# Expansion tiles of one or two PSUM banks out of one four-bank ring, in the first phase of a ConvNeXt-V2 block

## Chip, cores, metric

One core of one Trainium2 chip. The metric is the device time of one execution in microseconds (us), median of several runs. Each experiment is compared with runs of the kernel before that were taken beside it, so the median of before differs a little from place to place (1559.86 to 1561.48 us). "TensorE", "ScalarE", "VectorE" and "POOL" are the engines that the profile calls PE, ACT, DVE and POOL; SP issues transfers.

## The reference

```python
# x: [1, 512, 512, 96], dw: [3, 3, 96], w1: [96, 384], w2: [384, 96], all bf16
out = depthwise_3x3(x, dw)
h = layernorm(out, axis=-1)
h = gelu(einsum('bhwc,ce->bhwe', h, w1))
gx = sqrt((h * h).sum(axis=(1, 2)) + 1e-6)          # over the whole image
nx = gx / (gx.mean(axis=-1) + 1e-6)
h = grn_gamma * (h * nx) + grn_beta + h
return x + einsum('bhwe,ec->bhwc', h, w2)
```

The sum of squares over the whole image cuts the kernel in two. Phase 1 makes the convolution, the layer norm, the expansion to 384 channels and the gelu, and gathers the sums. Phase 2 makes the second product and the output. The change touches phase 1 only.

## The kernel before

The image is worked through in 128 blocks of four rows. One slot of the phase-1 loop does the convolution of one block and the expansion of an earlier one. A helper records every instruction in program order on its engine, so nearly every profile line names line 32 of the kernel; the tile names tell the lines apart.

The kernel's matmuls put their results into tiles in PSUM. The kernel lays it out as eight banks of 512 f32 per partition (in the trace, `Y` is 128x1536 f32 and a `U` 128x1024 f32): one for the statistics (`SG`, with the layer norm sums `S` and the Gram sums), three for the convolution (`Y`, a single buffer), four for the expansions (`U`, two buffers of two banks).

```python
psS = tile_pool(name="psS", bufs=1, space=PSUM)      # SG
psU = tile_pool(name="psU", bufs=2, space=PSUM)      # U: two tiles of two banks
psY = tile_pool(name="psY", bufs=1, space=PSUM)      # Y: three banks
# ... cut
def burst(n, fence=True):                            # a third of the convolution: 24 matmuls of 64 rows x 32 columns
    # ... cut: matmuls into Y
    if n < 2 and fence:
        pe.drain()

def evac():                                          # frees Y
    act.activation(out=y[:], in_=Y3[:], func=Identity)
# ... cut
def pair(j):                                         # two banks of the expansion, one gelu
    U = psU.tile([128, 2, QW], f32, name="U")
    for t in range(2):
        cm_mm(U[:, t, :], j, t)                      # 128x128 weights, 512 columns
    act.activation(out=gsh[:, :, j, :], in_=U[:], func=Gelu_apprx_tanh)
# rest(n): two banks as well, into gm; squares(j): bn_stats of a gelu's output on VectorE

conv(0); pair(0); conv(1); spread_out(); turn_x(s + 2)
pair(1); squares(0); gram_of_last(0)
pair(2); squares(1); gram_of_last(1)
rest(0); squares(2); conv(2); evac()
rest(1); stage_stats(b2)
rest(2); squares_rest()
```

So a slot has three conv bursts, six gelus over two banks each and one evacuation over three banks. A framework turns uses of tiles into semaphore waits; nothing in the kernel writes a wait by hand.

Of the kernel before, what the change touches and what calls it, by code (L numbers as in the profile page):

```python
# [53 lines left out]
def kernel(  # L54
# [20 lines left out]
    NI = C // 32  # L75
# [12 lines left out]
    def is_res(q):  # L88
        return q >= NBLK - RES
# [70 lines left out]
    with ExitStack() as p1:  # L160
# [2 lines left out]
        gmpool = p1.enter_context(tc.tile_pool(name="gm", bufs=3))  # L163
        bstpool = p1.enter_context(tc.tile_pool(name="bst", bufs=2))
        psS = p1.enter_context(tc.tile_pool(name="psS", bufs=1, space=bass.MemoryType.PSUM))
        psU = p1.enter_context(tc.tile_pool(name="psU", bufs=2, space=bass.MemoryType.PSUM))
        pc = p1.enter_context(ExitStack())
        psY = pc.enter_context(tc.tile_pool(name="psY", side="right", bufs=1, space=bass.MemoryType.PSUM))
        xinpool = pc.enter_context(tc.tile_pool(name="xin", side="right", bufs=4))
# [84 lines left out]
        def recompute_units(q):  # L254
            nk = kept_quads(q)
            ynt = grp[q]["ynt"]

            def fresh(j):
                if j == 0:
                    grp[q]["made"] = late.gr.tile([128, NCH, (NQ - 1) * QW], bf16, name="gr")  # L260
                if is_res(q):
                    U = psU.tile([128, 2, QW], f32, name="U")
                else:
                    U = late.psU2.tile([128, NQ - 1, QW], f32, name="U2")
                for t in range(nk, NQ):
                    pe.matmul(quad_out(U[:, t - nk, :]), lhsT=w1p[:, j * 128:(j + 1) * 128],
                               rhs=quad(ynt[:], t), start=True, stop=True)
                n = (NQ - nk) * QW
                act.activation(out=grp[q]["made"][:, j, :n], in_=U[:].rearrange("p k w -> p (k w)")[:, :n],
                                func=ACTF.Gelu_apprx_tanh)  # L270

            return [lambda j=j: fresh(j) for j in range(NCH)]
# [69 lines left out]
                pe.matmul(J[:, k % NI, :], lhsT=zrow[:, :128], rhs=zrow[:], start=True, stop=True)  # L342

        busy(FILL[0])
        Ud = psU.tile([128, 2, W], f32, name="U")[:, 0, :NI * 9].rearrange("p (i k) -> p i k", i=NI)
        for i in range(NI):
            dve.tensor_copy(out=dwx[:, i], in_=dw9[:, None, chans(i)].to_broadcast([9, GR, 32]))
            pe.matmul(Ud[:, i, :], lhsT=dwx[:, i].rearrange("p q c -> p (q c)"), rhs=ident_b[:9, :9],
# [38 lines left out]
        def turn_x(b):  # L387
            xin = xins.pop(b)
            t = xt_ring[b % NXT]
            pairs = t[:, 0:2, :].rearrange("p i s -> p (i s)").bitcast(f32)  # L390
            dve.transpose(out=pairs.rearrange("p (g m) -> p g m", m=MB),
                          in_=xin[:, :, 0:64].bitcast(f32))
            dve.transpose(out=t[:, 2, :].rearrange("p (g m) -> p g m", m=MB), in_=xin[:, :, 64:96])
# [13 lines left out]

        def conv_taps(b, spare):
            if spare:
                Ua = psU.tile([128, 2, W], f32, name="U")  # L410
                Ub = psU.tile([128, 2, W], f32, name="U")
                Y = [Ua[:, 0, :], Ua[:, 1, :], Ub[:, 0, :]]
            else:
                Y3 = psY.tile([128, NI, W], f32, name="Y")
                Y = [Y3[:, i, :] for i in range(NI)]
            mms = []
            for n in range(3):
                mms.append([(h, j, (n + h) % NI, dx) for dx in (0, -1, 1) for j in range(GR) for h in range(2)])
            flat = [m for ms in mms for m in ms]
            first = {}  # L420
            last = {}
            for n, (h, j, i, dx) in enumerate(flat):
                first.setdefault((i, j), n)
                last[i, j] = n

            def burst(n, fence=True):
                k = sum(len(ms) for ms in mms[:n])
                for h, j, i, dx in mms[n]:
                    src = b + shift(h, j)
                    o0, o1 = max(0, -dx), W - max(0, dx)  # L430
                    pe.matmul(
                        Y[i][32 * j:32 * j + 32, o0:o1],
                        lhsT=Wq[64 * h:64 * h + 64, i, dx + 1, j, :],
                        rhs=x_rows(src, 64 * h, 64 * h + 64, i, MB * (1 + dx) + o0, o1 - o0)
                        if 0 <= src < NBLK else zrow[64 * h:64 * h + 64, o0:o1],
                        start=first[i, j] == k,
                        stop=last[i, j] == k,
                    )
                    k += 1
                if n < 2 and fence:  # L440
                    pe.drain()

            def evac():
                y = ypool.tile([128, NI, W], bf16, name="y_bf")
                if spare:
                    act.activation(out=y[:, 0:2, :], in_=Ua[:], func=ACTF.Identity)
                    act.activation(out=y[:, 2, :], in_=Ub[:, 0, :], func=ACTF.Identity)
                else:
                    act.activation(out=y[:], in_=Y3[:], func=ACTF.Identity)
                ybf[b] = y  # L450

            return [lambda fence=True, n=n: burst(n, fence) for n in range(3)], evac
# [83 lines left out]
        def stage_spread(k):  # L536
            n = BATCHES[k][1]
            wide = rns.pop(k)
            U = psU.tile([128, 2, W], f32, name="U")
            for bb in range(n):  # L540
                for g in range(NG):
                    pe.matmul(U[:, bb, g * 128:(g + 1) * 128],
                              lhsT=wide[:, bb, g].rearrange("p j c -> p (j c)"), rhs=ident_b[:],
                              start=True, stop=True)
            rbc = rbcpool.tile([128, BATCH, W], bf16, name="rbc")
            act.activation(out=rbc[:, :n, :], in_=U[:, :n, :], func=ACTF.Identity)
            rbcs[k] = rbc
# [63 lines left out]
        def mlp_units(b):  # L611
# [4 lines left out]
            def cm_mm(dst, j, t):  # L616
                pe.matmul(quad_out(dst), lhsT=w1p[:, j * 128:(j + 1) * 128], rhs=quad(yt[:], t), start=True, stop=True)

            def pair(j):
                U = psU.tile([128, 2, QW], f32, name="U")  # L620
                for t in range(2):
                    cm_mm(U[:, t, :], j, t)
                act.activation(out=gsh[:, :, j, :], in_=U[:], func=ACTF.Gelu_apprx_tanh)

            def rest(n):
                U = psU.tile([128, 2, QW], f32, name="U")
                Uf = U[:].rearrange("p k w -> p (k w)")
                c0 = 2 * QW * n
                c, end = c0, c0 + 2 * QW
                while c < end:  # L630
                    if c < px0(b):
                        j, sz = c // QW, QW
                        cm_mm(Uf[:, c - c0:c - c0 + sz], j, 2)
                    else:
                        k, e0 = divmod(c - px0(b), E)
                        sz = min(E - e0, 512 - c % 512, end - c)
                        t, r = divmod(k, GR)
                        col = (cm_quads(b) + t) * 128
                        pe.matmul(Uf[:, c - c0:c - c0 + sz], lhsT=yt[:, r, col:col + 128], rhs=w1p[:, e0:e0 + sz],
                                  start=True, stop=True)  # L640
                    c += sz
                act.activation(out=gms[b][:, c0:end], in_=Uf, func=ACTF.Gelu_apprx_tanh)
# [16 lines left out]
            def store():  # L659
                sp.dma_start(out=g_dram[b], in_=gsh[:, 0].rearrange("p j w -> p (j w)"))  # L660

            return pair, rest, squares, squares_rest, store

        def gram_mms(b, part=None):
            n = (TAIL - px0(b)) // E
# [56 lines left out]
        for s in range(last_slot + 1):  # L722
# [26 lines left out]
            def spread_out():  # L749
                for k in get("spread"):  # L750
                    stage_spread(k)
                for b in get("norma"):
                    stage_norm(b)
# [24 lines left out]
                    gram_mms(b)  # L778
            else:
                b = mlp[0]  # L780
                pair, rest, squares, squares_rest, put_out = mlp_units(b)
                conv = lambda n, fence=True: taps[n](fence) if taps else None

                def gram_of_last(part):
# [1 line left out]
                        if b2 != b:  # L786
                            gram_mms(b2, part)

                conv(0)
                pair(0)  # L790
                conv(1)
                spread_out()
                if s + 2 < NBLK:
                    turn_x(s + 2)
                pair(1)
                squares(0)
                if not taps:
                    gram_of_last(0)
                    gram_of_last(1)
                if taps:  # L800
                    gram_of_last(0)
                pair(2)
                squares(1)
                if taps:
                    gram_of_last(1)
                rest(0)
                squares(2)
                for k in get("turn"):
                    stage_turn(k)
                conv(2)  # L810
                if evac:
                    evac()
                rest(1)
                for b2 in get("stats"):
                    stage_stats(b2)
                rest(2)
                squares_rest()
                for b2 in get("gram"):
                    if b2 == b:
                        gram_mms(b2)  # L820
# [125 lines left out]
```

## Time and profile before

| | before |
|---|---|
| median (first 3 runs) | 1561.48 us |
| slots with convolution, evacuation to evacuation (median) | 7.40 us |
| last evacuation / first addition of phase 2 starts at | 934.9 us / 1027.3 us |
| granted TensorE clock, whole run | 0.991 |

The windows of 300 to 800 us, the kernel before: for each engine busy us and, in brackets, instructions; then the granted clock, the share of the DMA engines and GB/s.

```profile
300.00:800.00 500.00, 465.69 (x8223) 225.53 (x8216) 477.04 (x803) 465.38 (x469) 449.39 (x328) 1.00 0.77 236
```

The order is TensorE, weight loads, VectorE, ScalarE, POOL. TensorE and ScalarE are each idle for about 7%, VectorE for less than 5%. A kernel like this has no single bounding engine, so the waits come next. The waits of ScalarE and of TensorE in the same stretch (waiting engine and tile, what it waited for, us in total, times, longest):

```profile
ACT gsh L32 <- PE U L32: 34.5, 71, 1.5
```

```profile
PE Y L32 <- ACT y_bf L32: 13.4, 66, 0.4
PE SG L32 <- DVE SG L32: 5.0, 4, 1.6
```

ScalarE waits once a slot, in front of one gelu; TensorE waits once a slot, for the evacuation. One slot in the timeline (start, length, engine, instruction, count, and in brackets the idle time before and what ended it), ScalarE and then TensorE:

```profile
598.24 1.47 ACT L32 ACTIVATE y_bf<-Y 128x1536 bf16<-128x1536 f32 x1
599.57 1.97 ACT L32 ACTIVATE gm<-U 128x1024 bf16<-128x1024 f32 x2
601.45 1.02 ACT L32 ACTIVATE gsh<-U 128x1024 bf16<-128x1024 f32 x1
602.91 1.94 ACT L32 ACTIVATE gsh<-U 128x1024 bf16<-128x1024 f32 x2 [0.44 <-PE U L32]
604.74 1.03 ACT L32 ACTIVATE gm<-U 128x1024 bf16<-128x1024 f32 x1
605.64 1.47 ACT L32 ACTIVATE y_bf<-Y 128x1536 bf16<-128x1536 f32 x1
```

```profile
599.76 0.89 PE L32 MATMUL Y<-xT,Wq 64*32 64x512 bf16 x24 [0.20 <-ACT y_bf L32]
600.76 0.60 PE L32 MATMUL U<-ynT,w1p 128*128 128x512 bf16 x2
601.29 0.87 PE L32 MATMUL Y<-xT,Wq 64*32 64x512 bf16 x24
602.27 0.60 PE L32 MATMUL U<-ynT,w1p 128*128 128x512 bf16 x2
...
604.51 0.88 PE L32 MATMUL Y<-xT,Wq 64*32 64x512 bf16 x24
605.32 0.39 PE L32 MATMUL U<-ynT,w1p 128*128 128x512 bf16 x1
```

Read as a loop: the evacuation ends at 599.71, conv 0 starts at 599.76, the first pair at 600.76, conv 1 at 601.29, the second pair at 602.27. Its gelu starts at 602.91, and after two more gelus the next evacuation starts at 605.64 and ends at 607.11. That is 7.40 us. Conv 0 and conv 1, which end in a drain, take 1.00 and 0.98 us until the next instruction starts; conv 2, without one, takes 0.81.

### The profile page before, as it was taken

What the parts mean: (1) busy time and instruction counts of PE and PEld (TensorE: products, weight loads), DVE (VectorE), ACT (ScalarE), POOL (GpSimd) and SP (SyncE); (2) the same over time, 40 slices, a digit from 0 to 9 for tenths busy, and PEclk for the clock granted to TensorE, in tenths of its full rate; (3) what the DMA queues carried; (4) which work ended last, traced back from release to release, by engine and by line L of the source; (5) the groups of instructions that cost most, each with busy time, mean ns of one, the idle gap of its engine ahead of it and who ended that gap; (6) DMA issues with size and microseconds to landing.
All of it is one profiled execution on the core that took longest, in us unless ns stands there. A gap on an engine that the chain in (4) does not pass through costs nothing. (4 is left out here: it accounts for less than half of the span.)

```text
span 1559.3 us, 54608 instructions
## 1 busy us (share of the span) xinstructions
PE 1438.9 (92%) x23119; PEld 819.7 (53%) x23119; DVE 1211.7 (78%) x2157; ACT 1436.7 (92%) x1306; POOL 1318.4 (85%) x933
## 2 busy tenths in 40 slices
PE   7889989999999999999999997789999999999998
PEld 3334444444444444444444443357777766676666
DVE  6749989999999999999999999955555555455555
ACT  3779989999999999999999999999999999899997
POOL 3459889989998998898899897459999999899997
PEclk8899999999999999999999999999999999999999
DMA  5568787777778778778868767879999999999996
GB/s 152 162 174 256 241 251 249 223 225 246 228 245 250 231 226 258 237 221 250 244 207 252 221 198 222 275 249 395 380 385 384 381 377 378 341 389 379 376 379 236
DMA packets 235467, 427.86 MB, mean 274 GB/s; under 512 B 34103, under 2 KB 148375, under 8 KB 235223
## 3 DMA queue, kind: packets, MB, share of 16 engines
q1 hardware_dynamic: 219972, 356.59, 70.4%
q0 software_dynamic: 13888, 67.64, 11.5%
q8 instruction: 181, 2.97, 0.8%
q14 instruction: 64, 0.52, 0.1%
q10 hardware_dynamic: 1362, 0.15, 0.1%
HBM read 272.78 MB, written 150.72 MB: 272 GB/s over the span
## 5 line engine op out<-in xcount | busy, mean ns | idle before, releaser
L32 PE MATMUL U<-ynT,w1p 128*128 128x512 bf16 x2292 | 664.4, 381 | 48.5 <-ACT gm L32 10.0
L32 ACT ACTIVATE gr<-U 128x1536 bf16<-128x1536 f32 (+1 forms) x384 | 519.1, 1456 | 13.1 <-PE U L32 11.3
L32 DVE BATCH_NORM_STATS2 bst<-gsh 128x6 f32<-128x512 bf16 x756 | 463.0, 674 | 21.7 <-ACT gsh L32 15.7
L32 DVE TENSOR_TENSOR o_sb<-O,xb 128x384 bf16<-128x384 f32 x512 | 277.9, 556 | 250.7 <-PE O L32 153.0
L32 POOL TENSOR_TENSOR yn<-y_bf,rbc 128x1536 bf16<-128x1536 bf16 x128 | 397.4, 3107 | 87.3 <-ACT rbc L32 31.0
L32 ACT ACTIVATE gsh<-U 128x1024 bf16<-128x1024 f32 x378 | 374.5, 1025 | 61.5 <-PE U L32 61.4
L278 POOL TENSOR_TENSOR xb<-xr,B2c 128x1536 f32<-128x1536 bf16 x126 | 394.8, 3135 | 33.9 <-DVE B2c L32 30.9
L32 ACT ACTIVATE gm<-U 128x1024 bf16<-128x1024 f32 x384 | 381.8, 1047 | 0.2
L32 PE MATMUL Y<-xT,Wq 64*32 64x511 bf16 (+1 forms) x8694 | 324.6, 391 | 32.9 <-ACT y_bf L32 25.8
L32 POOL TENSOR_TENSOR ysq<-y_bf 128x1536 bf16<-128x1536 bf16 x114 | 313.2, 2748 | 32.9 <-ACT y_bf L32 32.4
L32 PEld LDWEIGHTS <-w1p 128*128 128x128 bf16 x2292 | 181.6, 97 | 289.5 <-issue 203.3
L32 PEld LDWEIGHTS <-gr 128*128 128x128 bf16 x4584 | 236.8, 98 | 107.5 <-issue 23.4
L32 PE MATMUL O<-W2s,gr 128*128 128x96 bf16 x4584 | 257.2, 206 | 12.4 <-DVE o_sb L32 11.9
L32 DVE BATCH_NORM_STATS2 bst<-gm 128x6 f32<-128x512 bf16 x378 | 242.3, 679 | 29.7 <-ACT gm L32 29.7
L32 PEld LDWEIGHTS <-Wq 64*32 64x32 bf16 x9216 | 114.0, 91 | 212.5 <-issue 174.1
L32 ACT ACTIVATE y_bf<-Y 128x1536 bf16<-128x1536 f32 x121 | 177.5, 1467 | 16.2 <-PE Y L32 16.1
L32 DVE STREAM_TRANSPOSE xT<-xin 128x576 f32<-128x576 f32 (+1 forms) x256 | 180.4, 745 | 2.1 <-DMA xin<-in_x_dram 2.0
L32 PEld LDWEIGHTS <-gm 128*128 128x128 bf16 x1560 | 106.8, 98 | 66.3 <-issue 11.7
L32 PE MATMUL SG<-gm 128*128 128x128 bf16 x1560 | 126.1, 219 | 8.9 <-DVE SG L32 8.2
L32 PE MATMUL U<-w1p,ynT 128*128 128x384 bf16 (+2 forms) x780 | 126.5, 272 | 5.0 <-ACT gm L32 3.8
L250 POOL DMA_DIRECT2D xr<-in_x_dram x123 | 68.4, 556 | 35.9 <-POOL xb L278 35.9
L32 PEld LDWEIGHTS <-ynT 128*128 128x128 bf16 x780 | 67.3, 97 | 35.3 <-issue 15.4
(103 smaller groups left out, 696.6 us busy)
## 6 DMA issues: line engine op xcount, KB each, us to landing
ynT<-yn_dram SPq DMA_DIRECT2D x254, 384.0 KB
xin<-in_x_dram SPq DMA_DIRECT2D x126, 432.0 KB
yn_dram<-yn SPq DMA_DIRECT2D x512, 96.0 KB
xr<-in_x_dram POOLq DMA_DIRECT2D x128, 384.0 KB, 6.5
out_dram<-o_sb SPq DMA_DIRECT2D x127, 384.0 KB
g_dram<-gsh SPq DMA_DIRECT2D x126, 384.0 KB
gl<-g_dram SPq DMA_DIRECT2D x84, 384.0 KB
gl<-g_dram POOLq DMA_DIRECT2D x42, 384.0 KB, 7.2
```

What stands on the lines that cost most here:

```text
L32: r = f(*a, **k)
L250: pq.dma_start(out=xr[:], in_=x[0, r0:r0 + GR].rearrange("r w c -> (r w) c").rearrange("(p g) c -> p g c", g=PXP))
L278: pq.tensor_tensor(out=xb[:], in0=grp[q]["xr"][:], in1=bias[:, None, :].to_broadcast([128, PXP, C]), op=ALU.add)
```

## The change

The intent is to keep the same four banks but hand them out singly. Three banks can then be expanded before conv 1, and ScalarE can start on one bank while TensorE fills the next. The slot becomes 2, 1, conv, 1, 2, 2, conv, evacuation, 2, 1, 1 (banks per gelu): eight gelus for six. The drain after conv 1 is dropped.

```diff
-        psU = p1.enter_context(tc.tile_pool(name="psU", bufs=2, space=bass.MemoryType.PSUM))
+        psU = p1.enter_context(tc.tile_pool(name="psU", bufs=1, space=bass.MemoryType.PSUM))
+        NB = 4
+        ring = psU.tile([128, NB, W], f32, name="U")
+        next_bank = [0]
+
+        def banks(n):
+            k = next_bank[0] % NB
+            if k + n > NB:
+                k = 0
+            next_bank[0] = k + n
+            return ring[:, k:k + n, :]
 ... every psU.tile([128, 2, ...]) becomes banks(2)
-            def pair(j):
-                U = psU.tile([128, 2, QW], f32, name="U")
-                for t in range(2):
-                    cm_mm(U[:, t, :], j, t)
-                act.activation(out=gsh[:, :, j, :], in_=U[:], func=ACTF.Gelu_apprx_tanh)
+            def unit(bank, n):
+                U = banks(n)
+                if bank < 2 * NCH:
+                    j, t0 = divmod(bank, 2)
+                    for t in range(t0, t0 + n):
+                        cm_mm(U[:, t - t0, :], j, t)
+                    act.activation(out=gsh[:, t0:t0 + n, j, :], in_=U, func=ACTF.Gelu_apprx_tanh)
+                    return
 ... (rest(n) becomes the other half of unit)
+                if taps:
+                    conv(0)
+                    unit(0, 2)
+                    unit(2, 1)
+                    squares(0)
+                    conv(1, False)
 ... spread_out, turn_x
+                    unit(3, 1)
+                    unit(4, 2)
+                    squares(1)
+                    gram_of_last(0)
+                    unit(6, 2)
+                    squares(2)
 ... turn
+                    conv(2)
+                    evac()
+                    gram_of_last(1)
+                    unit(8, 2)
+                    unit(10, 1)
+                    unit(11, 1)
+                    squares_rest()
 ... stage_stats; slots without convolution use six units of two banks
```

More of the change, by code (lines that the diff above doesn't have):

```diff
@@ L261, in fresh @@
                 if is_res(q):
-                    U = psU.tile([128, 2, QW], f32, name="U")
+                    U = banks(2)
                 else:
@@ L268, in fresh @@
                 n = (NQ - nk) * QW
-                act.activation(out=grp[q]["made"][:, j, :n], in_=U[:].rearrange("p k w -> p (k w)")[:, :n],
+                act.activation(out=grp[q]["made"][:, j, :n], in_=(U if is_res(q) else U[:]).rearrange("p k w -> p (k w)")[:, :n],
                                 func=ACTF.Gelu_apprx_tanh)
@@ L344 @@
         busy(FILL[0])
-        Ud = psU.tile([128, 2, W], f32, name="U")[:, 0, :NI * 9].rearrange("p (i k) -> p i k", i=NI)
+        Ud = banks(2)[:, 0, :NI * 9].rearrange("p (i k) -> p i k", i=NI)
         for i in range(NI):
@@ L409, in conv_taps @@
             if spare:
-                Ua = psU.tile([128, 2, W], f32, name="U")
-                Ub = psU.tile([128, 2, W], f32, name="U")
+                Ua, Ub = banks(2), banks(2)
                 Y = [Ua[:, 0, :], Ua[:, 1, :], Ub[:, 0, :]]
@@ L445, in evac @@
                 if spare:
-                    act.activation(out=y[:, 0:2, :], in_=Ua[:], func=ACTF.Identity)
+                    act.activation(out=y[:, 0:2, :], in_=Ua, func=ACTF.Identity)
                     act.activation(out=y[:, 2, :], in_=Ub[:, 0, :], func=ACTF.Identity)
@@ L538, in stage_spread @@
             wide = rns.pop(k)
-            U = psU.tile([128, 2, W], f32, name="U")
+            U = banks(2)
             for bb in range(n):
@@ L617, in cm_mm @@
                 pe.matmul(quad_out(dst), lhsT=w1p[:, j * 128:(j + 1) * 128], rhs=quad(yt[:], t), start=True, stop=True)
-            def pair(j):
-                U = psU.tile([128, 2, QW], f32, name="U")
-                for t in range(2):
-                    cm_mm(U[:, t, :], j, t)
-                act.activation(out=gsh[:, :, j, :], in_=U[:], func=ACTF.Gelu_apprx_tanh)
-            def rest(n):
-                U = psU.tile([128, 2, QW], f32, name="U")
-                Uf = U[:].rearrange("p k w -> p (k w)")
-                c0 = 2 * QW * n
-                c, end = c0, c0 + 2 * QW
+            def unit(bank, n):
[6 more added lines that the diff above has]
+                    return
+                Uf = U.rearrange("p k w -> p (k w)")
+                c = c0 = (bank - 2 * NCH) * QW
+                end = c0 + n * QW
                 while c < end:
@@ L660, in store @@
                 sp.dma_start(out=g_dram[b], in_=gsh[:, 0].rearrange("p j w -> p (j w)"))
-            return pair, rest, squares, squares_rest, store
+            return unit, squares, squares_rest, store
         def gram_mms(b, part=None):
@@ L780 @@
                 b = mlp[0]
-                pair, rest, squares, squares_rest, put_out = mlp_units(b)
+                unit, squares, squares_rest, put_out = mlp_units(b)
                 conv = lambda n, fence=True: taps[n](fence) if taps else None
@@ L787, in gram_of_last @@
                             gram_mms(b2, part)
-                conv(0)
-                pair(0)
-                conv(1)
-                spread_out()
-                if s + 2 < NBLK:
-                    turn_x(s + 2)
-                pair(1)
-                squares(0)
-                if not taps:
+                if taps:
[4 more added lines that the diff above has]
+                    conv(1, False)
+                    spread_out()
+                    if s + 2 < NBLK:
+                        turn_x(s + 2)
+                    unit(3, 1)
[4 more added lines that the diff above has]
+                    squares(2)
+                    for k in get("turn"):
+                        stage_turn(k)
+                    conv(2)
[5 more added lines that the diff above has]
+                    squares_rest()
+                    for b2 in get("stats"):
+                        stage_stats(b2)
+                else:
+                    unit(0, 2)
+                    unit(2, 2)
+                    spread_out()
@@ L798 @@
                     gram_of_last(0)
                     gram_of_last(1)
-                if taps:
-                    gram_of_last(0)
-                pair(2)
-                squares(1)
-                if taps:
-                    gram_of_last(1)
-                rest(0)
-                squares(2)
-                for k in get("turn"):
-                    stage_turn(k)
-                conv(2)
-                if evac:
-                    evac()
-                rest(1)
-                for b2 in get("stats"):
-                    stage_stats(b2)
@@ L816 @@
-                rest(2)
-                squares_rest()
+                    squares(0)
+                    unit(4, 2)
+                    squares(1)
+                    for k in get("turn"):
+                        stage_turn(k)
+                    unit(6, 2)
+                    squares(2)
+                    unit(8, 2)
+                    for b2 in get("stats"):
+                        stage_stats(b2)
+                    unit(10, 2)
+                    squares_rest()
                 for b2 in get("gram"):
```

## The prediction

> **What bounds the kernel now.** The activity table by slices shows two phases: blocks with a convolution until about 940 us, a tail of expansions without convolution until about 1010 us, then the output phase. The change touches the first two. In the timeline a steady block lasts 7.40 us (evacuation to evacuation; few differ by over 0.1 us). No engine is full: in the windows table from 140 to 940 us, VectorE is busy 94.7%, ScalarE 92.9%, POOL 89.8%, and the waits of ScalarE are nearly all one wait: 54.1 us in 113 waits, gelu of the second pair waiting for its matmuls, 0.44 us a block.
>
> That wait closes a loop which I can add up to the measured period: end of the evacuation of Y (one Y buffer) -> +0.05 conv 0 with its drain 1.00 -> first pair 0.53 -> conv 1 0.98 -> second pair 0.60 until its end -> +0.04 gelu 0.92, 0.91, 0.90 (starts to starts) -> evacuation 1.47 = 7.40 us. So a latency loop between TensorE and ScalarE is the limit.
>
> **What the change does.** It keeps four PSUM banks, but hands them out singly, so three banks (1.5 tiles) are expanded before conv 1, and the single banks let ScalarE start earlier. The loop becomes: 0.05 + conv 0 1.00 + three banks about 0.75 + conv 1 without its drain 0.81 (as conv 2 takes now) + one bank 0.39 + 0.04 + gelu 0.50 + 0.92 + 0.92 + evacuation 1.47 = 6.85 us, an estimate from the same rows. It adds two ACTIVATEs per block (8 for 6). [...]0.60 us for 512 elements, 1.02 for 1024, 0.92 from start to start. [...] The removed drain saves TensorE about 0.17 us (0.98 against 0.81); its floor is about 6.8. Matmuls, transfers, VectorE and POOL work stay; VectorE needs about 7.05 to 7.1 per block, POOL 6.8 with the gaps in its short chains.
>
> So the loop stops being the limit, and ScalarE, VectorE and nearly POOL come to theirs together. With bursts (aggregation 2.8 us per 11 blocks, moments once in 4) they do not all reach it: the wait of the Gram matmuls for VectorE's clearing of SG (7.5 us in all now) should grow. I expect 7.15 to 7.2 us, 0.25 us less, for about 113 blocks: 28 us. The tail without convolution (5.55 us a block) is already ScalarE-bound without gaps and keeps its tile sizes: no change.
>
> **Predicted: 1533 us**, 8 in 10 between 1516 and 1550. Chances: faster by over 2% 0.42, within 2% 0.55, slower by over 2% 0.03.
>
> **What would show it.** Steady block 7.1 to 7.2 us; the 0.44 us wait of ScalarE almost gone (under 15 us in all); ScalarE busy 97% or more in that stretch; single-bank gelus near 0.60 us; VectorE waits under 0.15 us a block. If the block stays at 7.3 or more and ScalarE waits moved to another gelu, bank waits or VectorE's backlog took the gain.
>
> **What would make it wrong.** The dependencies of the shared ring tile tracked coarser than by bank; a stall of TensorE once in four blocks that grows as VectorE lags[...].

The three durations are in the trace of before: 0.60 us for ACTIVATEs of 512 elements (`rbc<-U`, mean 598 ns), 1.02 for gelus of 1024 (`gsh<-U`, mean 1025 ns), 0.92 from start to start. The floors of TensorE, VectorE and POOL are estimates, close to their busy time of 742.14, 757.73 and 718.56 us in the 800 us from 140 to 940 us (6.86, 7.01 and 6.65 us in 7.40). The sum came to this: the loop falls to 6.85 us and no longer limits; by the floors, a slot takes 7.15 to 7.2 us; 0.25 us less in about 113 slots is 28 us, and 1561 less 28 is 1533 us.

## The result, and the profile after

Ratios are the mean time of one kernel's runs over the mean of the other's runs of the same rounds, so they are not quite the ratios of the medians that stand beside them. All outputs are right.

| | before | after |
|---|---|---|
| median | 1561.45 us (4 runs) | 2526.57 us (2513.58 to 2530.38, 4 runs) |
| ratio, 95% interval | | 1.617 (1.611 to 1.623) |
| evacuation to evacuation, median | 7.40 us | 15.7 us (quartiles 13.5 and 16.1) |
| last evacuation starts at | 934.9 us | 1796.9 us |
| first addition of phase 2 starts at | 1027.3 us | 1995.7 us |
| granted clock, whole run | 0.991 | 0.756 |

The change made the kernel 62% slower. Of the 968 us by which phase 2 starts later, 862 are lost up to the last evacuation and 106 in the slots without convolution that follow. Phase 2 itself takes as long as before.

The windows of 300 to 800 us, the changed kernel:

```profile
300.00:800.00 500.00, 345.89 (x4188) 136.45 (x4173) 250.38 (x401) 262.98 (x302) 223.41 (x163) 0.71 0.39 121
```

TensorE, VectorE and POOL ran about half as many instructions as before in the same 500 us (ScalarE, which has more and smaller gelus in a slot, 302 for 469), and ScalarE fell from 93% to 53% busy. The granted clock fell from 1.00 to 0.71. The waits of ScalarE and TensorE there:

```profile
ACT gsh L32 <- PE U L32: 156.3, 130, 3.2
ACT gm L32 <- PE U L32: 67.2, 100, 1.2
...
```

```profile
PE U L32 <- ACT gsh L32: 79.3, 99, 1.3
PE U L32 <- ACT gm L32: 70.8, 66, 1.7
```

The second fence points to the cause. Before, no expansion waited for a gelu in this stretch. Now TensorE waits 165 times for a gelu, in front of expansions (`PE U`), for 150 us. ScalarE waits for expansions 230 times, for 224 us. Two engines that each wait for the other's last instruction are taking turns. One slot shows it, ScalarE (the first three quarters of the slot) and then TensorE (the first half):

```profile
1004.26 1.02 ACT L32 ACTIVATE gsh<-U 128x1024 bf16<-128x1024 f32 x1 [2.62 <-PE U L32]
1005.96 0.60 ACT L32 ACTIVATE gsh<-U 128x512 bf16<-128x512 f32 x1 [0.68 <-PE U L32]
1007.91 0.60 ACT L32 ACTIVATE gsh<-U 128x512 bf16<-128x512 f32 x1 [1.35 <-PE U L32]
1009.61 1.02 ACT L32 ACTIVATE gsh<-U 128x1024 bf16<-128x1024 f32 x1 [1.10 <-PE U L32]
1011.78 1.02 ACT L32 ACTIVATE gm<-U 128x1024 bf16<-128x1024 f32 x1 [1.15 <-PE U L32]
```

```profile
1001.55 1.48 PE L32 MATMUL Y<-xT,Wq 64*32 64x512 bf16 x24
1003.15 1.03 PE L32 MATMUL U<-ynT,w1p 128*128 128x512 bf16 x2
1005.34 0.59 PE L32 MATMUL U<-ynT,w1p 128*128 128x512 bf16 x1 [1.16 <-ACT gsh L32]
1005.86 1.48 PE L32 MATMUL Y<-xT,Wq 64*32 64x512 bf16 x24
1007.27 0.61 PE L32 MATMUL U<-ynT,w1p 128*128 128x512 bf16 x1
1008.56 1.01 PE L32 MATMUL U<-ynT,w1p 128*128 128x512 bf16 x2 [0.69 <-ACT gsh L32]
```

The pair at 1003.15 fills banks 0 and 1. The single expansion at 1005.34 fills bank 2, which nothing holds. It nevertheless starts 0.06 us after the gelu of banks 0 and 1 ended (1004.26 + 1.02 = 1005.28). In the same way the pair at 1008.56 (banks 0 and 1) follows the end of the gelu of bank 3 at 1008.51.

The compiled program says the same. For each first matmul of an expansion, this is the bank it writes, and the gelu whose completion its semaphore wait names (one slot of the changed kernel, same order as in the code):

```
expansion writes bank   waits for the gelu that read bank
0, 1                    3        (needed: 0, 1, three gelus earlier)
2                       0, 1     (needed: 2)
3                       2        (needed: 3)
0, 1                    3
2, 3                    0, 1
0, 1                    2, 3
2                       0, 1
3                       2
```

Every expansion waits for the gelu just before it; in the trace of the slot, five of the eight waits can be seen, and the other three are hidden behind other matmuls (the gelus that they name end at 1001.64, 1006.56 and 1012.80 us, before TensorE comes to those expansions at 1003.15, 1007.27 and 1013.66). In the kernel before, every pair waits for the gelu two pairs back, the last reader of its own tile. So the framework seems to treat the ring as one object, which the experiments test: such a ring is a single buffer, however many banks it has. The waits guard the whole tile, not the bank in use.

There is a second difference between the two slots. The conv burst took 1.48 us for 0.89, and the pair 1.03 for 0.60. The windows of 2 us over this slot, the changed kernel, TensorE alone (length, busy and instructions, granted clock, DMA share, GB/s):

```profile
1002.00:1004.00 2.00, 1.88 (x26) 0.50 0.01 4
1006.00:1008.00 2.00, 1.88 (x25) 0.50 0.03 8
...
1016.00:1018.00 2.00, 1.31 (x36) 1.00 0.96 324
```

The clock is 0.50 or 1.00, and 0.50 for most of the slot (of the five windows left out, four have 0.50, and one that holds both has 0.84). This slot alone can't tell how much of the loss is the waiting and how much is the clock, nor which causes which.

### The profile page after: what moved, and what is told of

Read it like the earlier page. It is cut to its first block, busy times and chain, and to the rows that moved or that the text cites. A ratio compares the mean times of both kernels' runs of the same rounds, so it can differ in the third digit from the quotient of the medians.

```text
span 2527.2 us, 54724 instructions
## 1 busy us (share of the span) xinstructions
PE 1879.0 (74%) x23119; PEld 919.4 (36%) x23119; DVE 1259.5 (50%) x2157; ACT 1544.5 (61%) x1534; POOL 1318.0 (52%) x933
## 4 chain that ended last, share of the span: by engine, by line
PE 59%; ACT 26%; POOL 6%; issue 3%; DMA 3%; DVE 1%; SPq 1%; ACTq 0%; POOLq 0%
PE U L32 32%; PE Y L32 15%; ACT gsh L32 13%; ACT gm L32 9%; PE O L32 7%; POOL xb L289 5%; PE SG L32 5%; ACT y_bf L32 4%; DMA yn_dram<-yn 2%; SPq L32 1%; DVE o_sb L32 1%; POOL gl L256 1%; DMA ynT<-yn_dram 1%; DMA xin<-in_x_dram 0%; POOL xr L261 0%
## 5 line engine op out<-in xcount | busy, mean ns | idle before, releaser
L32 PE MATMUL U<-ynT,w1p 128*128 128x512 bf16 x2292 | 862.3, 465 | 351.6 <-ACT gsh L32 299.5
L32 DVE BATCH_NORM_STATS2 bst<-gsh 128x6 f32<-128x512 bf16 x756 | 489.4, 680 | 641.3 <-ACT gsh L32 637.4
L32 ACT ACTIVATE gsh<-U 128x1024 bf16<-128x1024 f32 x492 | 406.2, 826 | 593.9 <-PE U L32 586.2
L32 ACT ACTIVATE gm<-U 128x1024 bf16<-128x1024 f32 x498 | 412.3, 828 | 277.7 <-PE U L32 275.0
L32 PE MATMUL Y<-xT,Wq 64*32 64x511 bf16 (+1 forms) x8694 | 453.9, 530 | 9.6 <-DVE B2bc_f L32 3.7
L32 PEld LDWEIGHTS <-w1p 128*128 128x128 bf16 x2292 | 207.1, 107 | 545.8 <-issue 484.3
L32 PE MATMUL U<-w1p,ynT 128*128 128x384 bf16 (+2 forms) x780 | 167.7, 306 | 262.6 <-ACT gm L32 260.4
L32 PEld LDWEIGHTS <-ynT 128*128 128x128 bf16 x780 | 85.1, 109 | 361.9 <-issue 344.2
L32 PEld LDWEIGHTS <-gm 128*128 128x128 bf16 x1560 | 147.0, 130 | 135.0 <-issue 129.5
L32 PE MATMUL SG<-gm 128*128 128x128 bf16 x1560 | 185.2, 282 | 0.0
```

The costliest lines, as they stand in the source:

```text
L32: r = f(*a, **k)
```

## The experiments

Theory A: the ring tile is one object to the waits, so TensorE and ScalarE take turns, and the low clock follows from TensorE's idle time. Theory B: the new order, the smaller tiles or the missing drain cost the time; the ring is only storage. Theory C: the low clock is a cause of its own, or TensorE's load lowers it.

### ring_only: the ring without the new order

```diff
  # the kernel before, its order (2, conv, 2, 2, 2, conv, evacuation, 2, 2) and its drains kept
-        psU = tile_pool(name="psU", bufs=2, ...)
+        ring = psU.tile([128, 4, W], f32, name="U")      # banks(n) as in the change
-                U = psU.tile([128, 2, QW], f32, name="U")
+                U = banks(2)
```

> The kernel before with its own order and its pairs, only that the pairs are slices of one four-bank tile. Theory A (the ring tile is one object for the waits, so every expansion waits for the gelu just before it, whatever bank it uses): about as slow as the change, 2150 to 2450 us, the granted clock under 0.85, and TensorE waits of near 1 us for the gelu just before in front of most expansions. Theory B (the new order, the smaller tiles and the missing drain are what costs; the ring is only storage): within 2% of before, 1530 to 1590 us.

Measured: 2108.33 us (2 runs), ratio 1.350. The waits of TensorE from 300 to 800 us, this kernel:

```profile
PE U L32 <- ACT gsh L32: 78.7, 117, 0.8
PE U L32 <- ACT gm L32: 71.8, 117, 1.1
```

Order, tile sizes, number of gelus and drains are those of before; pairs go alternately to banks 0, 1 and 2, 3, as they did in the two tiles. Only the object is one. The same waits appear and a slot takes 10.9 us for 7.40. Theory B does not explain this run. The time fell just short of the range given, the waits are shorter than expected (0.6 to 0.7 us on the mean), and the clock is higher (0.911): the turn-taking is costly even with little loss of clock.

### split_tiles: the new order without the ring

```diff
+        def banks(n):
+            if n == 2: U = psU.tile([128, 2, W], f32, name="UA")
+            else:      U = psU.tile([128, 1, W], f32, name="UC" or "UD", in turn)
-                    unit(6, 2)
+                    unit(6, 1); unit(7, 1)                # a pair can't span two tiles
```

> The changed order and the dropped drain, but the four banks are three separate tiles: one of two banks, two of one bank; where the changed kernel put a pair on the two single banks, two single expansions stand. Theory A: the false waits go, the clock stays near 0.99, and the time falls from 2527 to what was predicted at first, 1520 to 1560 us (nine gelus in a block[...]). Theory B: it stays over 2000 us.

Measured: 1543.05 us (4 runs), ratio 0.989 (0.987 to 0.991), clock 0.986; median slot 7.05 us. The order, the dropped drain and the bank sequence stay as in the change, except that one pair of a slot is split in two; each expansion now waits for the last gelu of its own tile alone. 984 us come back. This run and the one before it are the two halves of the change, and the ring half alone carries the loss.

The windows and TensorE's waits, 300 to 800 us, this kernel:

```profile
300.00:800.00 500.00, 468.71 (x8466) 236.72 (x8463) 488.08 (x831) 486.57 (x691) 464.46 (x345) 0.99 0.80 246
```

```profile
PE SG L32 <- DVE SG L32: 13.7, 7, 2.3
PE Y L32 <- ACT y_bf L32: 8.0, 49, 0.2
```

ScalarE's wait of 34.5 us is gone, VectorE is at 98%, and TensorE's largest wait is now for VectorE to clear the statistics bank: 13.7 us for 5.0 before. ScalarE has 10.7 us of waits left (7 waits, as many as TensorE has for the clearing); in a median slot it is busy for all of the 7.05 us.

### two_rings: a smaller dose

```diff
-        ring = psU.tile([128, NB, W], f32, name="U")
+        half = [psU.tile([128, 2, W], f32, name=f"U{i}") for i in range(2)]
-            return ring[:, k:k + n, :]
+            return half[k // 2][:, k % 2:k % 2 + n, :]     # (and a pair starts at an even bank)
```

> The changed order, with two tiles of two banks in place of the one of four; only the two single banks of one tile now share an object. Theory A: false waits remain in two places of a block (the second single bank behind the gelu of the first), so the time lies clearly between: 1600 to 1950 us. Theory B: no difference to the change, over 2300 us.

Measured: 1925.54 us (2 runs), ratio 1.233; median slot 10.6 us. TensorE's waits, 300 to 800 us, this kernel:

```profile
PE U L32 <- ACT gm L32: 98.5, 47, 2.1
PE U L32 <- ACT gsh L32: 8.1, 20, 0.6
```

Now one wait dominates. It comes once a slot and lasts 2.1 us: the last single bank behind the gelu of the other half of its tile, which stands behind the evacuation and a gelu of two banks. The dose decides, as theory A says, but so does the place: a single false wait near the evacuation holds up what follows it on TensorE, conv 0 and the first pair of the next slot (after the evacuation of 598.54 us ScalarE waits 2.10 us for that pair; before, it did not wait there). The clock was 0.83 in this stretch (0.93 in ring_only, whose slot is a little longer), so the clock does not go by the length of the slot alone. Nor does it go by the sum of TensorE's waits for gelus: 106.6 us here, 150.5 in ring_only and 150.1 in the change, at clocks of 0.83, 0.93 and 0.71. Which pattern of gaps lowers it stays open.

### ring_filled: the waits apart from the clock

```diff
  # the changed kernel
             def unit(bank, n):
+                if taps:
+                    for _ in range({2: 4, 4: 4, 6: 4, 10: 8, 11: 4}.get(bank, 0)):
+                        pe.matmul(SG[:, 2 * NS:], lhsT=zrow[:, :128], rhs=zrow[:, :NCH * 128],
+                                  start=False, stop=True, skip_group_check=True)    # adds zeros
```

> The changed kernel with matmuls of zero weights (128x384, added to the Gram sums, which they leave as they are) on TensorE where it waits for a gelu: 24 in a block with convolution. It tells the waits from the low clock. Theory A with the clock as a consequence: the granted clock rises to over 0.9 in that stretch and a block takes 12 to 14 us in place of 15.9 although TensorE has more to do: 2100 to 2350 us in all; what is left over 7.4 us a block is the false waits alone. Theory C (the low clock is a cause of its own, or TensorE's load lowers it): the clock stays at 0.7 or falls, and the time is the 2527 us of the change or more.

Measured: 2245.44 us (2 runs), ratio to before 1.438; it is 281 us faster than the change although TensorE executes 2736 more matmuls. The windows of 300 to 800 us, this kernel:

```profile
300.00:800.00 500.00, 452.80 (x5814) 225.81 (x5813) 294.89 (x476) 306.19 (x357) 267.92 (x200) 1.00 0.46 142
```

The clock is back at 1.00 and the median slot is 12.62 us (quartiles 12.61 and 12.63). So the low clock was a consequence of TensorE's idle time: work that computes nothing removed it (TensorE busy 452.80 us in 500 for 345.89, clock 1.00 for 0.71). Theory C falls. ScalarE's waits for expansions are still there: 275 in 500 us, 192.5 us in all (224 in the change). Of the 8.3 us that a median slot lost, about 5.2 (12.62 less 7.40) are the turn-taking at full clock and about 3.1 (15.7 less 12.62) are the clock. The added matmuls might themselves hold back an expansion, but the trace of the change, which has none, gives the same: between 300 and 800 us seven of its slots ran at a clock of 1.00 throughout, and they took 12.60 to 12.64 us. Two windows of the changed kernel, a slot of median length at a mean clock of 0.63 and the next one, at full clock:

```profile
463.68:479.38 15.70, 11.48 (x127) 4.41 (x126) 7.00 (x13) 7.93 (x9) 5.80 (x2) 0.63 0.22 69
479.38:492.00 12.62, 7.50 (x128) 3.46 (x125) 6.93 (x11) 7.72 (x9) 5.80 (x2) 1.00 0.63 197
```

The slots without convolution got no added matmuls. In the change the clock there was 0.53 (1850 to 1950 us); here the clock of the whole run, 0.958, lies below the 1.00 of the stretch.

### no_drain_1: the dropped drain alone

```diff
  # the kernel before
-                conv(1)
+                conv(1, False)
```

> The kernel before with one part of the change alone: no drain after conv 1 (its next accumulation is ordered by the waits for gelus between them). If the loop read from the profile of before (evacuation, conv 0, pair, conv 1, pair, three gelus, evacuation) is what sets 7.40 us, the 0.17 us that conv 1 is longer than conv 2 leave each block: 7.23 us a block, 1542 us. If VectorE or ScalarE sets the pace, or the drain costs nothing on the loop: 1558 to 1562 us.

Measured: 1545.42 us (6 runs), ratio 0.991 (0.989 to 0.992); median slot 7.23 us. This is the slot that the loop read from the profile of before gives (7.40 less 0.17). The loop was the limit of before, and a sixth of a microsecond on it counts in full. The total fell about 5 us less than the slot times 113 would give (14.4 for 19.2, against the runs of before beside it); TensorE's wait for the clearing grew from 5.0 to 9.2 us in 500. Dropping the drain after conv 0 as well was built too, but not run: the check before the chip refused it as a race, since it found nothing in the program that orders two matmuls that write the same bank of `Y`. What the chip would do there no run shows. Semaphore waits stand between conv 1 and conv 2.

### own_pairs: the new order in ordinary tiles

```diff
  # the changed kernel
-        ring = psU.tile(...) ; return ring[:, k:k + n, :]
+        psU = tile_pool(name="psU", bufs=2, ...)
+            U = psU.tile([128, 2, W], f32, name="U"); return U[:, 0:n, :]
-                    unit(10, 1); unit(11, 1)
+                    unit(10, 2)
```

> The changed order with ordinary tiles: every expansion takes a tile of two banks of its own from the two of before, and uses one or both banks; the last two single banks of a block are one pair (2, 1, conv, 1, 2, 2, conv, evacuation, 2, 2): 7 gelus. No false waits by construction. Theory A: near the first prediction, 7.2 us a block, 1540 us, clock 0.99. Theory B: far above before.

Measured: 1546.03 us (6 runs), ratio 0.991 (0.990 to 0.992); median slot 7.24 us, clock 0.994. A single bank costs a whole pair tile here, and yet it is as good as the dropped drain alone. The order does no harm; in this storage it brings little beyond the drain (7.24 us a slot for 7.23; with separate tiles it was 7.05).

### split_early, split_early_tail, pairs_early: what kept the separate tiles from the predicted time

```diff
  # split_tiles; the sums are read and cleared ahead of VectorE's last three statistics of the slot
-                    squares_rest()
                     for b2 in get("stats"):
                         stage_stats(b2)
+                    for k in at.pop((s + 1, "moments"), []):
+                        stage_moments(k)
+                    squares_rest()
  # split_early_tail: in the slots without convolution every second pair goes to two banks of Y
  # pairs_early: the first edit on own_pairs
```

> The changed order on three separate tiles again, and VectorE reads and clears the sums of the layer norm at the end of the block, ahead of its last three statistics, not at the start of the next block. With the separate tiles alone (1543 us) the steady block took 7.05 us but TensorE still waited 13.7 us in 500 (7 times, up to 2.3 us) for that clearing. If those stalls are what keeps the separate tiles from the predicted 1533 us, they go, and the time is 1522 to 1535 us. If VectorE (97.6% busy there) is simply full, nothing more comes: 1540 to 1545 us.

> The same, and the blocks without convolution take their second pair of banks from the convolution's own tile, which is free there: 6 gelus for 9 in ten blocks. About 3 us less than the run beside it, if ScalarE sets the pace there.

> The early clearing with the order in ordinary pairs (1546 us, 7.24 us a block, few stalls left there): ScalarE and TensorE bind it, so 1538 to 1546 us; less would say that VectorE's clearing held it up too.

Measured, each against the same nine runs of before (1560.60 us):

| | median | runs | ratio (95%) | median slot |
|---|---|---|---|---|
| split_early | 1525.62 us | 4 | 0.979 (0.977 to 0.981) | 7.04 us |
| split_early_tail | 1525.75 us | 5 | 0.978 (0.975 to 0.980) | 7.03 us |
| pairs_early | 1533.61 us | 4 | 0.983 (0.982 to 0.985) | 7.23 us |

The windows and TensorE's waits of split_early, 300 to 800 us:

```profile
300.00:800.00 500.00, 478.97 (x8664) 241.86 (x8649) 494.67 (x848) 495.89 (x706) 470.17 (x351) 1.00 0.82 251
```

```profile
PE Y L32 <- ACT y_bf L32: 7.3, 45, 0.2
PE SG L32 <- POOL ysq L32: 2.9, 3, 1.8
```

The wait for the clearing is gone, and ScalarE is busy 495.89 of 500 us, VectorE 494.67. The median slot hardly moved (7.05 to 7.04 us, while the mean between 300 and 800 us went from 7.27 to 7.10): the gain came from the few slots that had stalled. The tail's three microseconds could not be seen in the medians; in the profiled runs, the stretch from the last evacuation to the first addition of phase 2 is 2.0 us shorter (101.4 for 103.4). The expectation of pairs_early (1538 to 1546 us) was missed: it came in below, 12 us under own_pairs, so VectorE's clearing had held up that version as well. Both split versions beat the kernel before and the change; split_early_tail, whose whole interval lies below 0.98, is clearly over 2% faster than before. The early clearing was not tried on the kernel before or on no_drain_1, so how the 35 us of split_early divide between the order and the clearing is not shown. By the median slot, which the clearing hardly moved, the order with separate tiles gives 0.18 us beyond the dropped drain (7.23 to 7.05).

## Why the prediction was wrong

- **The loop that bounds the kernel before: right.** It was added up to 7.40 us. Taking 0.17 us out of it (no_drain_1) gave 7.23 us.
- **"It keeps four PSUM banks, but hands them out singly": the step that failed.** The program handed out slices of one tile, and the waits do not see slices. The "single banks let ScalarE start earlier" became "no expansion starts before the last gelu ends". In place of a slot of 7.15 to 7.2 us there was one of 15.7. The text named this among the things that would make it wrong, and rated "slower by over 2%" at 3%. It was hardly weighed, although the diff shows the one tile plainly.
- **The clock: absent from the sum.** The prediction took matmul durations as fixed. The idle time of turn-taking halved the clock for most of a slot (0.50 in six of the eight windows of the slot shown) and cost about 3.1 of the 8.3 us (ring_filled, and the slots of the change at full clock).
- **The gain once the waits go by the tile in use: right in kind, its size not.** split_tiles has what the prediction assumed, plus one gelu. It gained more in a median slot than forecast (7.05 us, for 7.15 to 7.2) and less in all (18 us for 28), since some slots stalled; split_early gained 35, with an edit that the prediction did not have. The 1543 us of split_tiles lie inside the range that was given for the change, which is no merit of the prediction: the change itself lay far outside it.
- **"The wait of the Gram matmuls for VectorE's clearing of SG should grow": right, for the kernel with separate tiles.** From 5.0 to 13.7 us in 500, and taking it away gave 1526 us.
- **The extra gelus: they cost less than estimated.** In a median slot before, ScalarE is busy for 6.96 us (7.40 less its wait of 0.44); in split_tiles, with three gelus more, for 7.05. That is 0.03 us each. From start to start the single banks of split_tiles take 0.48 us:

```profile
929.30 0.65 ACT L32 ACTIVATE gm<-UD 128x512 bf16<-128x512 f32 x1
929.78 1.08 ACT L32 ACTIVATE gsh<-UA 128x1024 bf16<-128x1024 f32 x1
930.68 0.67 ACT L32 ACTIVATE gsh<-UC 128x512 bf16<-128x512 f32 x1
```

(The timeline of split_tiles. Between 300 and 800 us the medians from start to start are 0.477 us for 512 elements and 0.903 to 0.920 for 1024, so two halves cost 0.03 to 0.05 us more than a whole.)

## What to carry to other kernels

Before you slice one tile into a ring of buffers, find out at what grain your framework waits. If it waits by tile, a ring in one tile is a single buffer (ring_only: 10.9 us a slot for 7.40), and separate tiles of the wanted sizes give the same memory with the intended waits (the same four banks took 2527 us in one tile and 1543 us in three). When a profile shows two engines each waiting for the other in front of most instructions, compare the buffer that the waiting instruction writes with the one that the awaited instruction read; if they differ, the wait is false. On TensorE such waits cost twice here: the idle time also lowered the granted clock, from 1.00 to 0.71 in 500 us, though no wait for a gelu was over 1.7 us, and stretched the matmuls that remain (a burst took 1.48 us for 0.89), which cost 3.1 of the 8.3 us a slot; filling the idle time with matmuls that compute nothing tells the two apart.
